# Layer A's queries and keys turned on VectorE as 32-bit pairs of heads, instead of on TensorE

## The chip, the cores and the metric

The kernel runs on one core of one Trainium2 chip. The metric is the device time of one launch in microseconds. The kernel before takes 3019.47 us, the median of three runs from 3016.03 to 3024.8.

## What is computed

Four layers run one after the other on x, a sequence of 2048 rows of 512 values, each with a layer norm ahead and a residual: A, B, A, B. Layer A is recurrent. It works on segments of 32 rows; ahead of each stand 8 memory rows, which are the first 8 output rows of the segment before.

```python
for s in range(n_seg):                      # 64 segments of 32 rows
    h = concatenate([mem, x[:, 32*s:32*s+32]], axis=1)      # 40 rows
    q, k, v = (einsum('btd,dhe->bhte', h, W) for W in (Wq, Wk, Wv))   # 32 heads of 128
    scores = einsum('bhqe,bhke->bhqk', q, k) * scale        # masked, softmax -> p
    o = einsum('bhqk,bhke->bhqe', p, v)
    o = einsum('bhte,hed->btd', o, Wo)
    mem = o[:, :8]
    outs.append(o[:, 8:])
```

Layer B is full softmax attention over the 2048 rows, 32 heads of 16.

## The kernel before, in words

Layer A's 64 segments follow each other, since each needs the memory rows of the one before. What TensorE does beside them is layer B's attention on rows that layer A has finished. The program writes TensorE's order itself: `segment` keeps a list of layer A's steps (`PLAN`, or `PLAN_PAIRS` when five or more units of layer B are due), a clock of its own estimates when each operand will be ready (`Clock`), and `step` picks each time among a step of layer A, a unit of layer B's attention (`emit_qk`, then `pv_mm`), or a piece of a chain (layer norm, projections of layer B). A quota of units, mostly 8 a segment, paces layer B; `PLACE` and `B_PLACE` set the segment positions at which the pieces of chains come due. What is left of layer B's attention when layer A ends runs in a tail, where ScalarE's exponentials are written to a ring (`fill`, L476, three tiles of 512 each, called fills below). Other engines take their instructions in the order in which this program emits them, and `evac_engine` and `evac16` choose VectorE or ScalarE for each copy out of PSUM by the same clock.

One segment, for each half of the heads (rr = 0, 1):

- Projections (`col_steps`, L737). 16 matmuls of 512 columns make Q, K or V of 16 heads. The array is used as four tiles of 32 columns, so four matmuls on different parts of W run side by side, each writing 32 PSUM partitions. Query row q of four heads then stands on partition 32t + q, with the head's 128 values along the free axis.
- The scores need Q and K with the 128 values on the partitions. `stage` copies the PSUM bank to a_qk as bf16 (L324 on ScalarE, L326 on VectorE). `turn` transposes its four pieces of 128x128 on TensorE against the identity into another bank (L761), using the full array. `qk_turn` copies that to a_QT or a_KT (`evac16`, L335 on ScalarE, L337 on VectorE). The steps are named X (Q) and Y (K) in the plan.
- The score group S (`s_group`, L795 and L801) adds the mask and multiplies, 32 matmuls of 40 columns. ScalarE takes the exponential (L805), VectorE sums, divides and transposes the probabilities (L808 to L817).
- `pv_group` or `pv_pair` (P, A, B in the plan, L824) multiplies by V, and `wo_steps` (W, L854) by Wo. L978 copies the memory rows into the next segment's input.

The last 8 rows of four segments are projected together, once in four segments, as a chain (`ln_chunk`): a_qkx, turned eight pieces at a time by the same `turn`, then a_QX and a_KX. GpSimd puts each segment's share into a_QP and a_KT (`rest_place`, L719 and L722).

The units of layer B use the array as four tiles of 32 rows for their first product (L588) and as column tiles for the second (L602). ScalarE takes their exponentials (L590 of three banks, L593 of one).

## Time and profile before

| | |
|---|---|
| median of three runs | 3019.47 us (3016.03 to 3024.8) |
| span of the profiled execution | 3016.9 us |
| TensorE busy | 2793.8 us |
| ScalarE busy | 2296.1 us |
| VectorE busy | 1787.0 us |
| GpSimd busy | 661.3 us |

The profile is of one execution; its own time is the span, from the first to the last instruction. Times are microseconds unless marked ns. PE is TensorE's matmuls, PEld its weight loads, DVE is VectorE, ACT is ScalarE, POOL is GpSimd. Line numbers (L761) are lines of the kernel before; a line can be a helper's, as L326, where every cast on VectorE is recorded. Matmuls are pipelined, so the duration of one (221 ns for a transpose) is longer than the distance to the next, and busy times of groups overlap.

### The profile page before, as it was taken

How to read it: one execution, taken by the hardware profiler on the slowest of the kernel's cores; microseconds unless marked ns; L12 is line 12 of the kernel's file. 1: busy time of each engine (PE TensorE's matmuls, PEld its weight loads, DVE VectorE, ACT ScalarE, POOL GpSimd, SP SyncE). 2: the span in 40 equal slices, each digit the busy share in tenths (PEclk: the TensorE clock that was granted, in tenths of full speed). 3: DMA queues.
4: the chain of work that ended last, by engine and by line, in shares of the span. 5: the costliest groups of instructions: out<-in, count | busy, mean ns of one | idle time of the engine just before them, and what ended most of it. 6: DMA issues, size and time to landing. Idle time of an engine off the chain costs nothing.

```text
span 3016.9 us, 153258 instructions
## 1 busy us (share of the span) xinstructions
PE 2793.8 (93%) x68190; PEld 1702.6 (56%) x68190; DVE 1787.0 (59%) x4836; ACT 2296.1 (76%) x2816; POOL 661.3 (22%) x1165
## 2 busy tenths in 40 slices
PE   5999999999999999999999999999999999998897
PEld 3666565655555555555656655555556555554463
DVE  2344646476666766577766667767666666654302
ACT  2555767587788788667787777778778899899996
POOL 2222222222222222203212212222222122221110
PEclk9999999999999999999999999999999999999998
DMA  6112224243444446435434433544452544555340
GB/s 255 50 47 77 87 82 122 83 136 114 141 123 142 136 118 192 125 106 171 131 99 123 123 91 116 149 140 129 120 170 81 171 125 131 182 168 159 104 120 14
DMA packets 281282, 373.74 MB, mean 124 GB/s; under 512 B 74105, under 2 KB 202305, under 8 KB 279073
## 3 DMA queue, kind: packets, MB, share of 16 engines
q1 hardware_dynamic: 222096, 186.25, 21.9%
q0 software_dynamic: 55040, 168.68, 17.6%
q8 instruction: 535, 8.77, 1.2%
q10 hardware_dynamic: 3472, 8.91, 0.8%
q14 instruction: 139, 1.13, 0.1%
HBM read 260.06 MB, written 103.55 MB: 121 GB/s over the span
## 4 chain that ended last, share of the span: by engine, by line
PE 62%; ACT 14%; DVE 9%; issue 8%; DMA 6%; POOL 1%; SPq 0%; DVEq 0%; ACTq 0%; POOLq 0%
PE bank L737 23%; PE bank L854 12%; ACT b_pr L476 7%; PE b_SX L588 6%; PE b_oacc L602 6%; PE bank L761 4%; ACT b_pt L590 3%; PE bank L824 3%; DMA b_W<-in_B_wqkv_dram 2%; ACT b_pt L593 2%; PE bank L801 1%; PE bank L1237 1%; PE bank L1283 1%; DMA a_Wq<-in_A_Wq_dram 1%; DVE a_qk L326 1%
## 5 line engine op out<-in xcount | busy, mean ns | idle before, releaser
L590 ACT ACTIVATE b_pt<-b_SX 128x1536 bf16<-128x1536 f32 (+1 forms) x877 | 1270.9, 1449 | 384.3 <-PE bank L588 354.6
L593 ACT ACTIVATE b_pt<-bank 128x512 bf16<-128x512 f32 (+1 forms) x877 | 523.2, 597 | 0.6 <-PE bank L588 0.6
L854 PE MATMUL bank<-a_OT,a_Wo 128*128 128x40 bf16 x16384 | 482.0, 180 | 24.3 <-ACT a_OT L324 18.4
L854 PEld LDWEIGHTS <-a_Wo 128*128 128x128 bf16 x16384 | 449.4, 96 | 67.2 <-issue 58.7
L737 PEld LDWEIGHTS <-a_hT 128*32 128x32 bf16 x12288 | 298.0, 96 | 294.9 <-issue 38.5
L588 PE MATMUL b_SX<-b_q,b_k 32*128 32x256 bf16 (+3 forms) x3870 | 353.0, 313 | 21.1 <-ACT b_pt L590 13.8
L588 PE MATMUL bank<-b_q,b_k 32*128 32x512 bf16 (+3 forms) x1290 | 337.0, 312 | 8.4 <-DVE a_V L326 2.5
L602 PE MATMUL b_oacc<-b_pt,b_v 128*17 128x512 bf16 (+3 forms) x5160 | 322.9, 314 | 11.0 <-DVE b_ain L1070 4.3
L326 DVE CAST a_OT<-bank 128x160 bf16<-128x160 f32 x778 | 216.7, 316 | 127.9 <-PE bank L824 125.1
L737 PE MATMUL bank<-a_Wv,a_hT 128*32 128x512 bf16 x4096 | 285.4, 383 | 1.7 <-DVE b_O L1330 1.3
L326 DVE CAST a_qk<-bank 128x512 bf16<-128x512 f32 x338 | 229.5, 681 | 84.2 <-PE bank L737 79.6
L737 PE MATMUL bank<-a_Wk,a_hT 128*32 128x512 bf16 x4096 | 271.8, 382 | 5.3 <-DVE a_hT L978 5.1
L737 PE MATMUL bank<-a_Wq,a_hT 128*32 128x512 bf16 x4096 | 275.5, 381 | 0.7 <-DVE a_V L326 0.4
L476 ACT ACTIVATE b_pr<-b_S 128x1536 bf16<-128x1536 f32 x202 | 270.9, 1876 | 1.1 <-PE b_S L473 1.1
L588 PEld LDWEIGHTS <-b_k 32*128 32x128 bf16 x5160 | 119.2, 91 | 193.7 <-issue 156.0
L1055 POOL DMA_DIRECT2D b_A<-b_ain x176 | 96.2, 546 | 595.8 <-DVE b_ain L1070 403.1
L1070 DVE TENSOR_TENSOR b_ain<-b_oacc,b_ain 128x512 f32<-128x512 f32 (+1 forms) x244 | 165.6, 679 | 91.9 <-PE b_oacc L602 88.0
L602 PEld LDWEIGHTS <-b_v 128*17 128x17 bf16 x6432 | 117.2, 88 | 163.0 <-issue 125.1
L761 PE MATMUL bank<-c_ident,a_qk 128*128 128x128 bf16 x2048 | 179.9, 221 | 23.1 <-DVE a_qk L326 12.7
L824 PE MATMUL bank<-a_PT,a_V 32*128 32x40 bf16 x3472 | 181.0, 177 | 15.3 <-DVE chk L351 3.4
L761 PEld LDWEIGHTS <-a_qk 128*128 128x128 bf16 x2048 | 119.6, 98 | 123.6 <-DVE a_qk L326 49.9
L808 DVE TENSOR_REDUCE a_sm<-a_pn 128x5 f32<-128x200 bf16 x256 | 92.4, 361 | 161.3 <-ACT a_pn L805 157.6
(156 smaller groups left out, 4103.1 us busy)
## 6 DMA issues: line engine op xcount, KB each, us to landing
b_ain<-b_A SPq DMA_DIRECT2D x232, 256.0 KB
b_W<-in_B_wqkv_dram POOLq DMA_DIRECT2D x192, 256.0 KB, 4.0
b_A<-b_ain POOLq DMA_DIRECT2D x176, 256.0 KB, 3.0
b_q<-b_Q SPq DMA_DIRECT2D x252, 128.0 KB
b_k<-b_K SPq DMA_DIRECT2D x199, 128.0 KB
b_v<-b_V SPq DMA_DIRECT2D x306, 68.0 KB
b_A<-b_aout POOLq DMA_DIRECT2D x80, 128.0 KB, 2.8
a_rest<-a_vx POOLq DMA_DIRECT2D x64, 128.0 KB, 2.7
```

The lines of the kernel that those rows point to most:

```text
L326: self.nc.vector.tensor_copy(dst, src)
L476: nc.scalar.activation(self.ring[:, s:s + n, :], self.sets[i][:, 0:n, :], ACT.Exp, scale=B_SCALE)
L588: nc.tensor.matmul(out[t][:, j * qw:(j + 1) * qw], lhsT=k[32 * t:32 * t + 32, kj * 128:(kj + 1) * 128], rhs=q[32 * t:32 * t + 32, j * u.ru ...
L590: nc.scalar.activation(pt[:, 0:NX, 0:w], self.SX[:, 0:NX, 0:w], ACT.Exp, scale=B_SCALE)
L593: nc.scalar.activation(pt[:, NX + i, 0:w], b.t[:, 0:w], ACT.Exp, scale=B_SCALE)
L602: self.nc.tensor.matmul(self.oacc[32 * t:32 * t + 17, j * step:j * step + qw], lhsT=u.v[:, kj, 17 * t:17 * t + 17], rhs=u.p[:, t, j * qw:( ...
L737: self.nc.tensor.matmul(b.t[32 * t:32 * t + 32, :], lhsT=lhsT(ft), rhs=W[:, ft, n * 512:(n + 1) * 512], start=(ft == 0), stop=(ft == 3), t ...
L761: self.nc.tensor.transpose(ps[:, 4 * i + j, :], x[:, 128 * j:128 * j + 128], self.ident[:])
L824: self.nc.tensor.matmul(ps[:, L * h4:L * h4 + L], lhsT=V[32 * t:32 * t + rows, st, h4 * DH:(h4 + 1) * DH], rhs=self.PT[32 * t:32 * t + row ...
L854: self.nc.tensor.matmul(ps[:, ft, :], lhsT=self.Wo[:, h, 128 * ft:128 * ft + 128], rhs=self.OT[:, h, :], start=(h == 0 and ft == 0), stop= ...
L1055: B.k.nc.gpsimd.dma_start(B.Acc_d[self.qc][self.hg][:, self.qo:self.qo + self.qw], acc[:, 0:self.qw])
L1070: nc.vector.tensor_tensor(acc[:, w], k.oacc[:, w], acc[:, w], ALU.add)
```

## The change

The columns of Wq and Wk are read in another order, so that one projection bank holds, on its partitions 32t to 32t + 31, the values 32t to 32t + 31 of 16 heads. The copy from PSUM writes the values of two heads alternately, so that two neighbouring bf16 form one 32-bit word. One VectorE transpose of 256 such words turns each 32x32 block, straight into a_QT, a_KT, a_QX or a_KX, now with two heads interleaved in their last axis. The score group reads Q and K with a step of two elements. The four transposes on TensorE, their PSUM bank and the copy out of it are gone, as are the steps X and Y of the plan; the two plans and the two tables of positions are written anew.

```diff
-PLACE = (-2.0, -1.5, -1.4, -1.4, -1.3, -0.5, -0.4, -0.4, 3.8)
-B_PLACE = (-2.7, -1.4, 0.4, 0.7, 1.7)
+PLACE = (-2.0, -1.6, -1.4, -1.1, -0.8, -0.5, -0.4)
+B_PLACE = (-4.3, -2.3, 0.1, 1.0, 2.1)
...
-        self.QT = bp.tile([128, 2, 4, 4, MAIN], bf16, name="a_QT")
-        self.KT = bp.tile([128, 2, 4, 4, L], bf16, name="a_KT")
+        self.QT = bp.tile([128, 2, 8, MAIN, 2], bf16, name="a_QT")
+        self.KT = bp.tile([128, 2, 8, L, 2], bf16, name="a_KT")
...
         def one(rr, w):
             def then(b, done):
-                t = self.lnp.tile([128, 512], bf16, name="a_qkx", tag="t", bufs=4)
-                b.free = self.evac(t[:], b.t[:], 512, done)
-                qk[w] = (t, b.free)
...
+                at = self.turn((self.QX, self.KX)[w][:, rr].rearrange("p i q b -> p i (q b)"), b, done)
+                if rr and w:
+                    self.at["X", ck] = at
...
-    def col_steps(self, W, lhsT, rr, ready, then):
+    def col_steps(self, W, lhsT, rr, ready, then, turned=False):
         st = {}
+        Wt = W[:].rearrange("p f (r i t c) -> p f r i t c", r=2, t=4, c=32)
...
-                self.nc.tensor.matmul(b.t[32 * t:32 * t + 32, :], lhsT=lhsT(ft), rhs=W[:, ft, n * 512:(n + 1) * 512],
-                                      start=(ft == 0), stop=(ft == 3), tile_position=(0, 32 * t))
+                out, rhs = b.t[32 * t:32 * t + 32, :], W[:, ft, n * 512:(n + 1) * 512]
+                if turned:
+                    out, rhs = out.rearrange("p (i c) -> p i c", c=32), Wt[:, ft, rr, :, t, :]
+                self.nc.tensor.matmul(out, lhsT=lhsT(ft), rhs=rhs, start=(ft == 0), stop=(ft == 3), tile_position=(0, 32 * t))
...
-    def stage(self, b, done):
-        t = self.stp.tile([128, 512], bf16, name="a_qk")
-        b.free = self.evac(t[:], b.t[:], 512, done)
-        return t, b.free
-
-    def turn(self, xs):
-
-        b, at = self.take()
-        ps = b.h(8, 128)
-        for i, (x, _) in enumerate(xs):
-            for j in range(4):
-                self.nc.tensor.transpose(ps[:, 4 * i + j, :], x[:, 128 * j:128 * j + 128], self.ident[:])
-        return b, self.ck.pe(0.224 * len(xs), max([at] + [r for _, r in xs]), "full", 4 * len(xs))
+    def turn(self, dst, b, done):
+
+        x = self.stp.tile([128, 8, 32, 2], bf16, name="a_qk")
+        b.free = self.evac(x[:].rearrange("p i c b -> p i b c"), b.t[:].rearrange("p (i b c) -> p i b c", b=2, c=32), 512, done)
+        self.nc.vector.transpose(dst.bitcast(i32), x[:].bitcast(i32).rearrange("p i c b -> p i (c b)"))
+        return self.ck.ew("DVE", 256, b.free)
...
-                    lhsT = self.QP[:, 4 * rr + t, j, :] if i else self.QT[:, rr, j, t, :]
-                    nc.tensor.matmul(ps[32 * t:32 * t + 32, 4 if i else j, :], lhsT=lhsT, rhs=self.KT[:, rr, j, t, :],
+                    lhsT = self.QP[:, 4 * rr + t, j, :] if i else self.QT[:, rr, 2 * t + j // 2, :, j % 2]
+                    nc.tensor.matmul(ps[32 * t:32 * t + 32, 4 if i else j, :], lhsT=lhsT, rhs=self.KT[:, rr, 2 * t + j // 2, :, j % 2],
...
-    PLAN = "K0 Q0 P1 Q1 Y0 X0 S0 W1 K1 W0 Y1 V0 X1 W3 W2 V1 S1 P0".split()
-    PLAN_PAIRS = "W1 Q0 W3 V0 Y0 K0 A1 X0 S0 X1 V1 K1 Q1 B0 Y1 A0 B1 S1 W0 W2".split()
+    PLAN = "S1 K0 Q0 K1 Q1 S0 W0 P0 W3 V0 V1 W2 P1 W1".split()
+    PLAN_PAIRS = "Q0 S0 K0 A1 B0 W3 K1 W1 Q1 V0 B1 V1 S1 W0 A0 W2".split()
```

`rest_place` keeps its two GpSimd copies, with the new layouts. The score group's masks, the softmax and everything after it are as before.

How the order moves, at two places. The first is TensorE in a segment with eight units (the 51st), from the projection that makes K of the first half (a_Wk) to the next unit of layer B. Before, the four transposes stand in between:

```order
L737 LDWEIGHTS a_hT
L737 MATMUL bank_242<-a_Wk,a_hT 32x512
...
L761 LDWEIGHTS a_qk
L761 MATMUL bank_243<-c_ident,a_qk 128x128
...
L588 LDWEIGHTS b_k
L588 MATMUL b_SX<-b_q,b_k 128x512
```

With the change:

```order
L730 LDWEIGHTS a_hT
L730 MATMUL bank_244<-a_Wk,a_hT 32x512
...
L588 LDWEIGHTS b_k
L588 MATMUL b_SX<-b_q,b_k 128x512
...
L602 LDWEIGHTS b_v
L602 MATMUL b_oacc<-b_pt,b_v 17x512
...
L771 LDWEIGHTS c_ident
L771 MATMUL bank_243<-c_hide,c_ident 32x200
```

The unit (L588, L602) follows the projection directly, and the score group (L771) comes after it.

The second place is VectorE in the same segment, from the first cast of Q or K to the first softmax. Before:

```order
L326 CAST a_qk<-bank_243 128x512
L1063 COPY b_aout<-b_oacc 128x256
L326 CAST a_V<-bank_244 128x512
L326 CAST a_qk<-bank_242 128x512
L337 COPY a_QT<-bank_243 128x512
L1070 TENSOR_TENSOR b_ain<-b_oacc,b_ain 128x512
L337 COPY a_KT<-bank_245 128x16x32
L326 CAST a_V<-bank_242 128x512
L808 TENSOR_REDUCE a_sm<-a_pn 128x5
```

With the change:

```order
L326 CAST a_qk<-bank_242 128x8x2x32
L746 STREAM_TRANSPOSE a_QT<-a_qk 128x256
L1031 COPY b_aout<-b_oacc 128x256
L326 CAST a_qk<-bank_243 128x8x2x32
L746 STREAM_TRANSPOSE a_KT<-a_qk 128x8x32
L326 CAST a_qk<-bank_244 128x8x2x32
L746 STREAM_TRANSPOSE a_KT<-a_qk 128x8x32
L784 TENSOR_REDUCE a_sm<-a_pn 128x5
```

Each cast is followed by its transpose, the copies out of the second bank are gone, and the two casts of V have left VectorE's queue here for ScalarE's.

## Rows read from the trace of the kernel before

**Rows 1.** The page's busy times: us, share of the span, instructions.
```profile
PE 2793.8 (93%) x68190; PEld 1702.6 (56%) x68190; DVE 1787.0 (59%) x4836; ACT 2296.1 (76%) x2816; POOL 661.3 (22%) x1165
```

**Rows 2.** Busy time of each engine in four stages of the span.
```profile
core 0: us, PE busy (x) PEld busy (x) DVE busy (x) ACT busy (x) POOL busy (x), PEclk, DMA share, GB/s
0.00:400.00 400.00, 345.95 (x9589) 225.34 (x9592) 177.55 (x539) 211.59 (x400) 90.14 (x163) 0.99 0.31 102
400.00:2400.00 2000.00, 1903.75 (x47839) 1156.89 (x47832) 1339.22 (x3593) 1525.03 (x1891) 469.51 (x823) 0.99 0.43 128
2400.00:2700.00 300.00, 282.36 (x6621) 161.76 (x6621) 188.69 (x493) 272.12 (x309) 65.98 (x116) 0.98 0.48 144
2700.00:3017.00 317.00, 261.79 (x4153) 158.57 (x4148) 81.50 (x212) 287.34 (x220) 35.64 (x63) 0.97 0.37 109
```

**Rows 3.** The chain that ended last: shares of the span by line.
```profile
by line: PE bank L737 22.9%; PE bank L854 12.3%; issue 8.2%; ACT b_pr L476 6.9%; PE b_SX L588 6.5%; PE b_oacc L602 5.5%; PE bank L761 4.2%; ACT b_pt L590 3.5%; PE bank L824 2.7%; DMA b_W<-in_B_wqkv_dram 2.2%; ACT b_pt L593 1.7%; PE bank L80
```

**Rows 4.** The same chain in order of time, one segment: start, length, what.
```profile
1003.53 1.29 PE bank L737 x24
...
1006.57 0.33 PE bank L761 x4
...
1007.88 0.98 PE bank L737 x16
...
1008.94 0.23 PE bank L801 x32
1009.17 0.32 PE b_SX L588 x3
...
1009.50 0.32 PE b_oacc L602 x4
...
1012.42 0.54 PE b_oacc L602 x8
1012.96 0.55 PE bank L761 x8
```

**Rows 5.** Groups by form, TensorE's transposes: busy us, mean ns; idle before, releaser.
```profile
L761 PE MATMUL bank<-c_ident,a_qk 128*128 128x128 bf16 x2048 | 179.9, 221 | 23.1 <-DVE a_qk L326 12.7 <-DVE a_xo L1204 5.3 <-ACT a_QX L335 3.4
L761 PE MATMUL bank<-c_ident,a_qkx 128*128 128x128 bf16 x512 | 39.6, 220 | 0.9 <-ACT a_qkx L324 0.7 <-issue 0.2
```

**Rows 6.** The same view, copies, casts and transposes on VectorE and ScalarE.
```profile
L326 DVE CAST a_qk<-bank 128x512 bf16<-128x512 f32 x338 | 229.5, 681 | 84.2 <-PE bank L737 79.6 <-ACT b_pt L590 0.2
L326 DVE CAST a_V<-bank 128x512 bf16<-128x512 f32 x204 | 140.3, 688 | 73.0 <-PE bank L737 72.1
L815 DVE STREAM_TRANSPOSE a_PT<-a_pn 128x256 bf16<-128x256 bf16 x256 | 113.7, 444 | 7.9
L337 DVE COPY a_KT<-bank 128x512 bf16<-128x512 bf16 x222 | 92.4, 416 | 68.5 <-PE bank L761 67.3
L337 DVE COPY a_QT<-bank 128x512 bf16<-128x512 bf16 x223 | 92.3, 414 | 4.1 <-ACT b_pt L593 3.0 <-PE bank L761 0.6
L337 DVE COPY a_KX<-bank 128x512 bf16<-128x512 bf16 x64 | 26.9, 420 | 46.4 <-PE bank L761 45.0
L326 DVE CAST b_vst<-bank 128x512 bf16<-128x512 f32 x32 | 21.7, 678 | 39.4 <-PE bank L1283 37.1 <-issue 1.1 <-ACT b_pt L590 1.0
L335 ACT COPY a_KT<-bank 128x512 bf16<-128x512 bf16 x34 | 20.1, 590 | 3.4 <-PE bank L761 3.3
L337 DVE COPY a_QX<-bank 128x512 bf16<-128x512 bf16 x47 | 19.4, 414 | 0.0
```

**Rows 7.** Source view of L761: what its engine was idle for.
```profile
its engine sat idle before it (us, times) until:
  DVE a_qk L326: 62.6, 163
```

**Rows 8.** Groups by form, the tail's exponentials on ScalarE.
```profile
L476 ACT ACTIVATE b_pr<-b_S 128x1536 bf16<-128x1536 f32 x201 | 270.4, 1879 | 1.1 <-PE b_S L473 1.1
```

More of the change, by code (lines that the diff above doesn't have):

```diff
@@ L129, in __init__ @@
         self.ring, self.stream, self.slot, self.fills, self.summed, self.more = None, deque(), 0, 0, 0, True
-        self.staged, self.pos, self.placed = {}, 0.0, -1
+        self.pos, self.placed = 0.0, -1
         self.first_xn, self.rush = None, False
@@ L691, in rest @@
             return self.col_steps(self.Wv, lambda ft: self.hX[:, ft, :], rr, self.w_at["V"], then)
-        qk = {}
         def one(rr, w):
             def then(b, done):
-                t = self.lnp.tile([128, 512], bf16, name="a_qkx", tag="t", bufs=4)
-                b.free = self.evac(t[:], b.t[:], 512, done)
-                qk[w] = (t, b.free)
-            return self.col_steps((self.Wq, self.Wk)[w], lambda ft: self.hX[:, ft, :], rr, max(self.at["x"], self.w_at["QK"[w]]), then)
-        def turn(rr):
-            b, done = self.turn((qk[1], qk[0]))
-            ps = b.h(8, 128)
-            self.evac16(self.KX[:, rr].rearrange("p j t q -> p j (t q)"), ps[:, 0:4], 512, done)
-            b.free = self.evac16(self.QX[:, 4 * rr:4 * rr + 4].rearrange("p t j q -> p t j q"), ps[:, 4:8].rearrange("p j (t q) -> p t j q", q=32), 512, done)
-            if rr:
-                self.at["X", ck] = b.free
-            return b.free
+                at = self.turn((self.QX, self.KX)[w][:, rr].rearrange("p i q b -> p i (q b)"), b, done)
+                if rr and w:
+                    self.at["X", ck] = at
+            return self.col_steps((self.Wq, self.Wk)[w], lambda ft: self.hX[:, ft, :], rr, max(self.at["x"], self.w_at["QK"[w]]), then, turned=True)
         plan = [4 * ck + x for x in PLACE] if ck else ()
         v = [lambda: rest(0), lambda: rest(1)]
-        x = [lambda: one(0, 0), lambda: one(0, 1), lambda: turn(0), lambda: one(1, 0), lambda: one(1, 1), lambda: turn(1)]
-        c = self.chain([pe] + (x + v if late else v + x), self.ck.t["PE"] + wait, modes="fccfccfcc" if late else "fccccfccf", plan=plan, gate=(6, 4 * ck - 1))
-        c.v_left = 1 if late else 7
+        x = [lambda: one(0, 0), lambda: one(0, 1), lambda: one(1, 0), lambda: one(1, 1)]
+        c = self.chain([pe] + (x + v if late else v + x), self.ck.t["PE"] + wait, modes="fcccccc", plan=plan, gate=(4, 4 * ck - 1))
+        c.v_left = 1 if late else 5
         return c
@@ L748, in cols @@
         return out
[L750 to L762 removed]
+    def turn(self, dst, b, done):
[3 more added lines that the diff above has]
+        return self.ck.ew("DVE", 256, b.free)
     def qk_steps(self, h_s, proj, rr):
         def then(b, done):
[L766 to L776 removed]
+            self.at["X", proj, rr] = self.turn((self.QT[:, rr], self.KT[:, rr, :, 0:MAIN, :])[proj].rearrange("p i q b -> p i (q b)"), b, done)
+        return self.col_steps((self.Wq, self.Wk)[proj], lambda ft: h_s[:, ft, :], rr, max(self.at.get("mem", 0.0), self.w_at["QK"[proj]]), then, turned=True)
     def v_steps(self, h_s, rr):
@@ L867, in a_ready @@
             t = max(at.get("mem", 0.0), self.w_at[k])
-        elif k in "XY":
-            p = "QK"[k == "Y"]
-            if f"{p}{g}" in left:
-                return INF
-            t = self.staged[p, g][1]
         elif k == "S":
-            if f"X{g}" in left or f"Y{g}" in left or at["R"] == INF:
+            if f"Q{g}" in left or f"K{g}" in left or at["R"] == INF:
                 return INF
@@ L887, in a_ready @@
         return max(t, self.bank_at())
-    MODE = {"Q": "PV", "K": "PV", "X": "full", "Y": "full", "S": "PV", "V": "PV", "P": "S", "A": "S", "B": "S", "W": "full"}
+    MODE = {"Q": "PV", "K": "PV", "S": "PV", "V": "PV", "P": "S", "A": "S", "B": "S", "W": "full"}
     def a_pick(self, left):
```

26 lines of the change are left out of this document (6 added, 20 removed).

## The prediction

> **What bounds the kernel now.** I read the busy shares first. TensorE is busy for 93% of the span, ScalarE for 76%, VectorE for 59% [rows 1]. A share over the whole span hides the stages, so the next view is the table by stage [rows 2]. In the first 400 us, where layer A runs almost alone, and from 400 to 2400 us, where units of layer B's attention are woven in, TensorE is busy 86% and 95% and ScalarE 53% and 76%. From 2400 to 2700 us ScalarE has come up to 91% and TensorE stands at 94%. After 2700 us, when layer A is over and only exponentials of layer B are left, ScalarE leads with 91%. So until about 2700 us the order in which TensorE gets through its list sets the time, and after that ScalarE does. The chain that ended last says the same: the projections (L737) and the output product (L854) lead it, and the transposes of Q and K (L761) hold 4.2% of it [rows 3], 127 us of 3016.9.
>
> The chain in order of time shows the price of one place [rows 4]. Four transposes stand for 0.33 us, eight for 0.55 us. So four more cost 0.22 us, and the remaining 0.11 us is what a change of the array's tiling costs (full array for transposes, column tiles for projections, row tiles for the units). Projections go at 0.98 us for 16, that is 0.245 for four matmuls with the change, and at 1.29 for 24, that is 0.215.
>
> **The change, part by part.**
>
> *Transposes on TensorE go.* 2048 of them on a_qk and 512 on a_qkx [rows 5], 640 fours at 0.22 us: **-141 us**.
>
> *Changes of tiling go.* Counted over TensorE's two orders up to the first fill of the tail, neighbours with different tilings fall from 3109 to 2637, because most fours stood between two projections or between a projection and a unit. 472 at 0.11 us: **-52 us**. Together 193 us. The bounds: the chain counts only 127 us, since some fours stood where something else was late anyway; the busy time of the two groups is 219.5 us [rows 5], which overlaps its neighbours. I take 193, the price at which the engine was seen to advance, and keep 127 and 219 as ends. The order shows no work put in the hole: the same projections and score groups follow, closer together.
>
> *The copies out of PSUM go, and VectorE transposes come.* 640 copies go, 556 of them on VectorE (222 + 223 + 64 + 47) at about 0.415 us, the other 84 on ScalarE at 0.59 [rows 6]. 640 transposes of 256 words come, all on VectorE. No row has a transpose of 32-bit words. The nearest is that of 256 bf16 elements, 0.444 us [rows 6]; below it stands a copy of 512 values at 0.414, above it twice the row, 0.89, if a 32-bit word should count as two. I take 0.444: 284 us come and 231 go. The orders also hand 97 casts of V from VectorE to ScalarE, 97 x 0.688 [rows 6] = 67 us off VectorE and 57 us on ScalarE, which loses 84 x 0.59 = 50 us of copies. Both engines end near where they were, and TensorE's path pays nothing while VectorE is at 67% in the long stage [rows 2]. If that cover goes, score groups wait: the second rival.
>
> *The cast with its values interleaved.* 640 casts keep their count of 512 and write every second bf16. The cast into b_vst writes in pieces of 16 and takes 0.678 us against 0.681 for the plain one [rows 6]. I take zero; twice the time would put 0.68 us on an engine that is not the bound.
>
> *The wait that is added.* A transpose follows its cast in VectorE's queue, and where the cast is on ScalarE (245 of 640) VectorE waits for another engine with softmax rows behind it. The orders put the softmax of an earlier score group ahead of such a transpose, so I price this at zero and leave it to the second rival. The waits before the old transposes, 62.6 us of weight-load idling on VectorE's a_qk [rows 7], may vanish or move to the score groups; on TensorE's own row only 23.1 us stood before them [rows 5]. I take "moves", and -23 us as the end.
>
> *Operands read with gaps.* Score groups read Q and K with a step of two elements, projections read Wq and Wk in 16 runs of 32 columns. No row has either. Taken as free; the bounds are in the third rival and, for the 256 score groups, 0.23 us once more each [rows 4], 59 us, if such a read ran at half pace.
>
> *Work that moves to the tail.* The new order runs 842 units beside layer A where the old one ran 865, 15 of the 23 missing in layer A's last 16 segments, and 232 fills in the tail instead of 201.3. This takes 23 x 2 x 0.21 us (four more matmuls of a unit's second product, 0.54 against 0.33 us [rows 4]) from TensorE's list, **-10 us**, and puts 30.7 fills of 270.4/201 = 1.345 us [rows 8] on ScalarE where ScalarE is the bound, **+41 us**.
>
> *ScalarE comes closer.* From 400 to 2400 us its 1525 us of work stay and the stage shrinks by some 140 us, so its share goes from 76 to about 82%. In the stage where it is at 91% TensorE's share is 1.1 points lower than in the long one [rows 2]. Between nothing and twice those 1.1 points of 2000 us, 44 us, I take **+20 us**.
>
> The sum is -141 - 52 - 10 + 41 + 20 = -142 us. The profiled execution spans 3016.9 us, 2.6 us under the median of the three runs, 3019.47; from the median the forecast is **2878 us**.
>
> **The rivals.**
>
> *ScalarE takes a large part back.* For it: 91% in the last stage, and segments that come without layer B's projections have the least TensorE work for the same eight units, so there ScalarE would end last. Against it: in the long stage it has a quarter to spare. Then TensorE's list gives only what the chain counted: 127 + 10 - 41 - 20 = 76 us, 2943 us.
>
> *VectorE is late with K and Q.* If a 32-bit transpose takes 0.89 us, or waits as long behind a cast on ScalarE, each of 256 score groups starts up to 0.44 us later, 113 us in all; 2991 us. For it: both transposes and the two casts of a group now stand in one queue, and the score group follows the last projection at a distance of one or two groups. Against it: VectorE's 67%. The Trainium skill speaks for this side too: "VectorE: DVE Perf Modes", Rules for kernel authors, says to transpose 128x128 on TensorE where a PSUM destination will do. The trace disagrees as far as it goes, since the engine that the page recommends is the one at 93%.
>
> *Slower: the projections' operand.* Each of the 2560 fours of matmuls on Wq and Wk now reads 16 runs of 32 columns instead of one of 512. If a run cost as much as four short matmuls of the score group, 0.23/8 = 0.029 us [rows 4], a four would take 0.46 us in place of 0.215 and the kernel 627 us more, 3505 us. It decides from 142/2560 = 0.055 us per four, a quarter more than now. For it: no row shows such a read. Against it: four projections that read at four addresses at once already run at 0.215 us for 512 columns, so the reads have slack in where they go. The Trainium skill bears on this: "SBUF — State Buffer", Door 1, says lines are 16 bytes and two hits in each suffice for full rate. By that rule neither the runs of 64 bytes nor the step of 4 bytes costs anything; no run here shows it.
>
> **How the numbers follow.** The forecast's own case, 2828 to 2915 us, has 0.62: its lower end takes 219 us for the transposes, no loss to ScalarE and the 23 us of waits (2878 - 26 - 20 - 23 is 2809, of which I keep the part that can come together). ScalarE's case has 0.20 and reaches to about 2970; VectorE's has 0.08; the projections' 0.07; that something else eats it all has 0.03. The range 2828 to 2950 holds the first and most of the second, 0.8 in all. About 0.3%, 9 us, is what a measurement of this kernel can tell from no change. Faster by more: 0.62 + 0.20 + 0.07 = 0.89. The same: 0.03. Slower: 0.08.
>
> **What would show it.** Right: no L761 rows; fours of projections still 0.215 us apart in the chain; 640 transposes on VectorE at about 0.44 us; layer A over some 180 us earlier, near 2520 us; 232 fills behind it, the tail 40 us longer; ScalarE near 82% in the long stage. ScalarE's case would show as PE waiting for b_pt or free b_SX before the units, VectorE's as score groups waiting for a_QT or a_KT, the projections' as a chain step above 0.27 us for four. The forecast is wrong if layer A's end comes less than 120 us earlier, or if the tail grows by more than 60 us.

## The result and the profile after

The changed kernel takes **2910.72 us**, the median of four runs (2906.69 to 2912.67), beside 3021.62 us for the kernel before, with one run more than the three ahead (3016.03 to 3024.8). The ratio is 0.9627, with an interval of 0.961 to 0.9644, a gain of some 111 us where 142 were forecast. The profiled execution spans 2908.7 us, 108.2 less than the span of before.

The page's busy times, engine by engine, answer to [rows 1]:

```profile
PE 2645.1 (91%) x65859; PEld 1586.6 (55%) x65859; DVE 1741.4 (60%) x4758; ACT 2335.4 (80%) x2876; POOL 667.4 (23%) x1165
```

TensorE lost 149 us of busy time. ScalarE has 39 us more work in a span that is 108 us shorter, and that is the first thing that was not in the forecast: there its casts and copies came to 57 - 50 = 7 us more, and the fills of the tail only do exponentials that units did beside layer A before.

The table of stages, cut where layer A's parts now end, answers to [rows 2]; its columns are as there:

```profile
0.00:400.00 400.00, 341.62 (x9931) 218.21 (x9934) 207.97 (x625) 219.84 (x391) 95.00 (x171) 0.98 0.32 104
400.00:2200.00 1800.00, 1677.01 (x43252) 997.90 (x43245) 1219.59 (x3323) 1463.39 (x1846) 448.02 (x778) 0.98 0.45 133
2200.00:2550.00 350.00, 328.03 (x8001) 189.10 (x7997) 228.76 (x594) 324.25 (x393) 85.29 (x148) 0.98 0.50 151
2550.00:2909.00 359.00, 298.42 (x4705) 181.40 (x4701) 85.05 (x218) 327.90 (x249) 39.08 (x69) 0.97 0.36 106
```

In the long stage TensorE has gone from 95% to 93% (1677 of 1800) and ScalarE from 76% to 81%. In the stage ahead of the tail they stand together, 94% and 93%. The granted clock in the long stage reads 0.98 where it read 0.99.

The chain that ended last, by line, answers to [rows 3]:

```profile
by line: PE bank L730 18.6%; PE bank L830 12.9%; issue 12.7%; ACT b_pr L476 7.8%; PE b_SX L588 5.7%; ACT b_pt L590 5.5%; PE b_oacc L602 4.8%; ACT b_pt L593 2.8%; PE bank L800 2.4%; DVE a_qk L326 1.8%; PE bank L1205 1.4%; DMA b_W<-in_B_wqkv_
```

The transposes (L761, 4.2%) are gone and nothing of TensorE stands in their place. The projections' own pace is as in [rows 4], 24 of them in 1.29 us, in the same chain in order of time:

```profile
917.11 1.29 PE bank L730 x24
```

Of the chain's work, what grew most is ScalarE's exponentials of layer B's units, L590 and L593, from 3.5 + 1.7 to 5.5 + 2.8 per cent, and a cast of Q and K on VectorE (L326) has come in with 1.8. What grew more than any work is "issue", time in which the engine that the chain passes through waited for nothing that the profile shows: 8.2 to 12.7 per cent, some 120 us. Its longest piece, 15.93 us from 1918.97, stands where the chain passes through GpSimd's queue. TensorE's own idle time grew by far less (below), so these shares say where the chain runs and not what was lost there.

Where layer A ends is seen from the source view of the copy of the memory rows, the last instruction of each segment. Before, and then after (min/median/max in ns, first and last start in us):

```profile
L978 DVE CAST a_hT<-bank x126: 178/191/192, 58.5 to 2679.2; 128x32 bf16<-128x32 f32 x126
```
```profile
L946 DVE CAST a_hT<-bank x126: 129/192/193, 54.8 to 2531.7; 128x32 bf16<-128x32 f32 x126
```

Layer A's last such copy comes 147.5 us earlier. From it to the end of the span it was 3016.9 - 2679.2 = 337.7 us and is now 2908.7 - 2531.7 = 377.0, so the tail grew by 39.3 us. The forecast had 183 us earlier and 41 us longer. All that it missed lies inside layer A.

Busy times up to that last copy, before and then after (columns as in [rows 2]):

```profile
0.00:2679.20 2679.20, 2512.76 (x63519) 1532.41 (x63523) 1694.04 (x4589) 1988.88 (x2574) 624.54 (x1100) 0.99 0.42 126
0.00:2531.70 2531.70, 2329.00 (x60734) 1395.12 (x60734) 1644.16 (x4506) 1990.12 (x2606) 626.13 (x1092) 0.98 0.44 131
```

So TensorE's busy time in layer A fell by 184 us, and its idle time (the stretch less the busy time) grew from 166.4 to 202.7, by 36 us. The forecast's terms for TensorE's work were -141 - 52 - 10 = -203, and +20 was its term for ScalarE coming closer, which would show as idle time. Of the 35 us that layer A ended too late, 19 are busy time that stayed and 16 are more idle time than forecast.

The groups by form show the new price of the casts and transposes; they answer to [rows 6], and the last row to [rows 8]:

```profile
L476 ACT ACTIVATE b_pr<-b_S 128x1536 bf16<-128x1536 f32 x232 | 312.1, 1895 | 3.5 <-PE b_S L473 3.4
L326 DVE CAST a_qk<-bank 128x512 bf16<-128x512 f32 x395 | 287.1, 727 | 81.6 <-PE bank L730 79.3
L324 ACT CAST a_qk<-bank 128x512 bf16<-128x512 f32 x245 | 183.1, 752 | 52.9 <-PE bank L730 45.2
...
L746 DVE STREAM_TRANSPOSE a_KT<-a_qk 128x256 int32<-128x256 int32 x256 | 113.0, 443 | 45.6 <-ACT a_qk L324 40.1
L746 DVE STREAM_TRANSPOSE a_QT<-a_qk 128x256 int32<-128x256 int32 x256 | 111.8, 437 | 24.7 <-ACT a_qk L324 20.1
L324 ACT CAST a_V<-bank 128x512 bf16<-128x512 f32 x149 | 89.6, 613 | 22.1 <-PE bank L730 21.4
```

For ScalarE's casts [rows 6] had no row; the same view of the kernel before has it:

```profile
L324 ACT CAST a_qk<-bank 128x512 bf16<-128x512 f32 x174 | 102.6, 590 | 58.1 <-PE bank L737 57.9
L324 ACT CAST a_V<-bank 128x512 bf16<-128x512 f32 x52 | 30.5, 586 | 13.8 <-PE bank L737 11.3 <-ACT a_pn L805 1.6
```

Two things are to be read here. The transpose of 256 words of 32 bits takes 0.443 and 0.437 us, what one of 256 bf16 took. The cast that writes every second bf16 is not free: 0.752 us on ScalarE against 0.590 for the plain one, 0.727 on VectorE against 0.681. That is 245 x 0.162 = 40 us more on ScalarE and 395 x 0.046 = 18 us on VectorE.

What TensorE's weight loads and matmuls were idle for is in the source views, of the units' first product (L588) and of the score group (L801, now L777). Before, the units, then the score group:

```profile
  ACT b_pt L590: 13.8, 47
...
  ACT b_pt L593: 1.7, 8
```
```profile
  ACT a_QT L335: 4.9, 13
  DVE a_QT L337: 3.1, 12
  DVE a_KT L337: 1.5, 8
```

After, in the same order:

```profile
  ACT b_pt L590: 30.4, 85
...
  ACT b_pt L593: 5.2, 23
```
```profile
  DVE a_QT L746: 24.3, 24
  DVE a_KT L746: 9.6, 22
```

The units wait for ScalarE 35.6 us instead of 15.5. The score groups wait for K and Q 33.9 us instead of 9.5. The source view adds up the idle time of two rows, matmuls and weight loads, and a weight load's idle time can lie beside a matmul. By this view the old transposes had 62.6 us ahead of them for VectorE's a_qk alone [rows 7], and 24.4 us more have come ahead of the score groups. By the row of matmuls alone 23.1 us stood ahead of the old transposes on a_qk [rows 5], and the score groups' first matmuls have 14.6 where L801 had 0.6:

```profile
L777 PE MATMUL bank<-a_KT,a_QT 128*32 128x40 bf16 x4096 | 71.1, 182 | 14.6 <-DVE a_QT L746 8.4 <-DVE ln_mv L372 3.5 <-DVE a_KT L746 2.0
```

So part of these waits moved to the score groups, about six tenths by the matmuls' row and four tenths or less by both rows.

The last view is TensorE's granted clock, the mean of each execution (before, then after):

```profile
core 0: 3016.9 us, clock 0.987
```
```profile
core 0: 2908.7 us, clock 0.981
```

The clock has two levels, 2.4 and 1.2 GHz, which the rows give as 1 and 0.5; a mean below 1 tells of stretches at the lower one. Stretches at 0.5 cost at most half of their length directly, which for a whole execution is one less the mean, times the span: 0.013 x 3016.9 = 39 us before, 0.019 x 2908.7 = 55 us after. Two of the falls, in the table of the stretches ahead of each and behind it (columns as in [rows 2]):

```profile
917.90:927.90 10.00, 8.59 (x176) 4.05 (x172) 9.05 (x24) 9.57 (x13) 3.45 (x6) 1.00 0.43 134
928.00:931.30 3.30, 3.30 (x80) 2.61 (x72) 3.20 (x11) 2.38 (x4) 2.04 (x4) 0.50 0.74 242
1576.70:1586.70 10.00, 8.33 (x336) 5.49 (x334) 6.80 (x21) 9.70 (x14) 1.67 (x4) 1.00 0.54 154
1586.80:1590.10 3.30, 3.30 (x114) 3.00 (x107) 1.18 (x5) 1.48 (x2) 0.54 (x1) 0.50 0.34 92
```

Ahead of each fall TensorE was busy for 8.6 and 8.3 of 10 us while ScalarE was busy for 9.6 and 9.7: TensorE was idle in small pieces, the longest wait 0.9 us in both stretches, in the first for VectorE's b_ain and in the second for ScalarE's b_pt. Behind it TensorE runs at 1.2 GHz, with no idle time left, until the clock comes back.

### The profile page after: what moved, and what is told of

It reads as the page before. It is cut to its first block, busy times and chain, and to the rows that moved or that the text cites. A ratio compares the mean times of both kernels' runs of the same rounds, so it can differ in the third digit from the quotient of the medians.

```text
span 2908.7 us, 148110 instructions
## 1 busy us (share of the span) xinstructions
PE 2645.1 (91%) x65859; PEld 1586.6 (55%) x65859; DVE 1741.4 (60%) x4758; ACT 2335.4 (80%) x2876; POOL 667.4 (23%) x1165
## 4 chain that ended last, share of the span: by engine, by line
PE 51%; ACT 18%; issue 13%; DVE 9%; DMA 5%; POOL 3%; POOLq 0%; DVEq 0%; ACTq 0%; SPq 0%
PE bank L730 19%; PE bank L830 13%; ACT b_pr L476 8%; PE b_SX L588 6%; ACT b_pt L590 5%; PE b_oacc L602 5%; ACT b_pt L593 3%; PE bank L800 2%; DVE a_qk L326 2%; PE bank L1205 1%; DMA b_W<-in_B_wqkv_dram 1%; DMA b_A<-b_ain 1%; PE bank L777 1%; ACT a_qk L324 1%; DVE ln_st L370 1%
## 5 line engine op out<-in xcount | busy, mean ns | idle before, releaser
L590 ACT ACTIVATE b_pt<-b_SX 128x1536 bf16<-128x1536 f32 (+1 forms) x854 | 1245.2, 1458 | 285.2 <-PE bank L588 261.3
L593 ACT ACTIVATE b_pt<-bank 128x512 bf16<-128x512 f32 (+1 forms) x854 | 516.7, 605 | 7.0 <-PE bank L588 7.0
L830 PE MATMUL bank<-a_OT,a_Wo 128*128 128x40 bf16 x16384 | 476.4, 180 | 22.1 <-issue 11.2
L730 PEld LDWEIGHTS <-a_hT 128*32 128x32 bf16 x12288 | 316.2, 96 | 283.2 <-issue 36.1
L588 PE MATMUL b_SX<-b_q,b_k 32*128 32x256 bf16 (+3 forms) x3732 | 344.9, 316 | 36.6 <-ACT b_pt L590 30.4
L588 PE MATMUL bank<-b_q,b_k 32*128 32x512 bf16 (+3 forms) x1244 | 329.8, 315 | 18.8 <-DVE b_xo L1339 7.5
L326 DVE CAST a_qk<-bank 128x512 bf16<-128x512 f32 x395 | 287.1, 727 | 81.6 <-PE bank L730 79.3
L602 PE MATMUL b_oacc<-b_pt,b_v 128*17 128x512 bf16 (+2 forms) x4976 | 317.9, 317 | 11.4 <-DVE b_ain L1038 4.7
L476 ACT ACTIVATE b_pr<-b_S 128x1536 bf16<-128x1536 f32 x232 | 312.1, 1895 | 3.5 <-PE b_S L473 3.4
L326 DVE CAST a_OT<-bank 128x160 bf16<-128x160 f32 x736 | 203.1, 313 | 179.1 <-PE bank L800 175.7
L730 PE MATMUL bank<-a_Wv,a_hT 128*32 128x512 bf16 x4096 | 270.3, 381 | 1.7 <-DVE a_xo L1172 1.2
L588 PEld LDWEIGHTS <-b_k 32*128 32x128 bf16 x4976 | 119.2, 92 | 255.9 <-issue 226.3
L324 ACT CAST a_qk<-bank 128x512 bf16<-128x512 f32 x245 | 183.1, 752 | 52.9 <-PE bank L730 45.2
L602 PEld LDWEIGHTS <-b_v 128*17 128x17 bf16 x6432 | 118.8, 89 | 168.0 <-issue 130.8
L195 POOL DMA_DIRECT2D b_W<-in_B_wqkv_dram x192 | 145.7, 761 | 245.2 <-PE bank L1205 125.0
L800 PEld LDWEIGHTS <-a_V 32*128 32x128 bf16 x4096 | 126.0, 91 | 101.3 <-issue 53.6
```

Source lines behind the costliest of these rows:

```text
L195: self.nc.gpsimd.dma_start(t[:], self.WB_src[:, :, col:col + 256])
L324: self.nc.scalar.copy(dst, src)
L326: self.nc.vector.tensor_copy(dst, src)
L476: nc.scalar.activation(self.ring[:, s:s + n, :], self.sets[i][:, 0:n, :], ACT.Exp, scale=B_SCALE)
L588: nc.tensor.matmul(out[t][:, j * qw:(j + 1) * qw], lhsT=k[32 * t:32 * t + 32, kj * 128:(kj + 1) * 128], rhs=q[32 * t:32 * t + 32, j * u.ru ...
L590: nc.scalar.activation(pt[:, 0:NX, 0:w], self.SX[:, 0:NX, 0:w], ACT.Exp, scale=B_SCALE)
```

## The experiments

Each kernel is compared by its ratio to the kernel before on the same chip, since the kernel before itself took 3021.62 to 3034.35 us on the chips used. Edits are against the changed kernel where nothing else is said.

**The cast, plain.** The cast writes its 512 values in a row, so that a word holds two neighbouring values of one head. Q and K are then in another order, and the scores are of other values.

```diff
-b.free = self.evac(x[:].rearrange("p i c b -> p i b c"), b.t[:].rearrange("p (i b c) -> p i b c", b=2, c=32), 512, done)
+b.free = self.evac(x[:].rearrange("p i c b -> p (i c b)"), b.t[:], 512, done)
```

> The changed kernel with one edit: the cast out of PSUM writes its 512 values in a row instead of every second bf16 (so Q and K hold their values in another order than the scores need; nothing else is left out). Theory A, the interleaved write is what the forecast missed: the cast of a_qk took 0.752 us on ScalarE and 0.727 on VectorE in the changed kernel, against 0.590 and 0.681 before; with the plain write they go back to those, 245 x 0.16 = 39 us leave ScalarE and 395 x 0.046 = 18 us VectorE, and since ScalarE paces the units the time falls by 20 to 40 us from 2910.7, to 2870 to 2890. Rival B, the casts lie beside other work and the missing 32 us went into waits of the new order (score groups close behind their projections): the casts get shorter, the time stays within 9 us of 2910.7.

**The cast, reading with gaps.** The interleaving is moved to the other side: the cast reads PSUM with a step of 32 words and writes in a row. The result is that of the change.

```diff
-b.free = self.evac(x[:].rearrange("p i c b -> p i b c"), b.t[:].rearrange("p (i b c) -> p i b c", b=2, c=32), 512, done)
+b.free = self.evac(x[:], b.t[:].rearrange("p (i b c) -> p i c b", b=2, c=32), 512, done)
```

> The changed kernel, but the cast reads PSUM with a step of 32 words and writes in a row (same result). If the cost lies in writing single bf16 with gaps, the casts go back to 0.59 and 0.68 us and the time goes where the plain cast's goes (theory A: 2870 to 2890; B: 2911). If any order with gaps costs the same on either side, the casts stay at 0.75 and 0.73 us and the time at 2911.

Measured: 2910.18 us, ratio 0.9577 (0.9548 to 0.9606), for the plain cast, and 2902.31 us, 0.9559 (0.9527 to 0.959), for the one that reads with gaps. Groups by form of the first and of the second:

```profile
L326 DVE CAST a_qk<-bank 128x512 bf16<-128x512 f32 x395 | 266.4, 675 | 85.8 <-PE bank L730 83.5
L324 ACT CAST a_qk<-bank 128x512 bf16<-128x512 f32 x245 | 144.9, 592 | 67.2 <-PE bank L730 67.1
```
```profile
L326 DVE CAST a_qk<-bank 128x512 bf16<-128x512 f32 x395 | 266.3, 674 | 83.5 <-PE bank L730 81.3
L324 ACT CAST a_qk<-bank 128x512 bf16<-128x512 f32 x245 | 144.9, 592 | 68.9 <-PE bank L730 68.1 <-PE bank L777 0.6
```

Gaps on the side that reads PSUM cost nothing, 592 and 674 ns, and gaps on the side that writes cost all of the difference. The kernel that reads with gaps does what the change does and is the fastest of this study: run again later it took 2899.32 us, 0.9561 (0.9544 to 0.9577), beside the change's 0.9627 (0.961 to 0.9644) and, in another run of it, 0.9618 (0.9596 to 0.9641). 0.0057 to 0.0068 of some 3030 us is 17 to 21 us for the interleaved write, with some 10 us of uncertainty by the intervals. The change and this kernel were never timed on the same chip. By their own times, 2910.72 and 2916.06 against 2902.31 and 2899.32, it is 8 to 17 us, and layer A's last copy comes at 2520.3 and 2525.2 us instead of 2531.7 and 2535.9, 11 us earlier in the mean. So the write costs **some 8 to 21 us**, a fifth to a half of the 40 us that it adds to ScalarE. The plain cast comes out lower: 0.0041 to 0.0050, 12 to 15 us, by the ratio, and nothing by its own time beside the change's first run. By the first it lies between its two expectations, by the second it is the rival's.

**Gaps in the projections' output or operand.** Could the projections interleave, and the cast be plain? In the first kernel they write PSUM with a step of two words, in the second they read the columns of W one by one, 256 bytes apart. Both use the plain cast.

```diff
-out, rhs = out.rearrange("p (i c) -> p i c", c=32), Wt[:, ft, rr, :, t, :]
+out, rhs = out.rearrange("p (i c b) -> p i b c", b=2, c=32), Wt[:, ft, rr, :, t, :].rearrange("p (i b) c -> p i b c", b=2)
```

> The changed kernel, but the projections of Q and K write PSUM with a step of two words, so that two heads are interleaved there already and the cast is plain (same result). If TensorE writes with that step at its full pace (fours of matmuls 0.215 us apart), the time is that of the plain cast. If the step costs TensorE, it shows in the distance of the fours: a half more, 0.11 us on 2560 fours, would be 275 us more than the plain cast, some 3160.

```diff
-out, rhs = out.rearrange("p (i c) -> p i c", c=32), Wt[:, ft, rr, :, t, :]
+out, rhs = out.rearrange("p (i c b) -> p i c b", b=2, c=32), Wt[:, ft, rr, :, t, :].rearrange("p (i b) c -> p i c b", b=2)
```

> The changed kernel, but the projections of Q and K read the weights' columns in the interleaved order (neighbouring columns 256 bytes apart), write PSUM in a row, and the cast is plain (same result). If TensorE reads single columns at any address at its full pace, the time is that of the plain cast. The third rival of the prediction in its hardest form: if such reads cost, a four takes up to twice 0.215 us, 2560 x 0.215 = 550 us more than the plain cast, some 3430.

Measured: 3378.99 us, ratio 1.112 (1.1086 to 1.1153), and 3504.59 us, 1.1541 (1.1507 to 1.1574). The source views of the projections (duration min/median/max in ns) of the change, of the first and of the second kernel:

```profile
L730 PE MATMUL bank<-a_Wk,a_hT x4096: 376/379/634, 39.0 to 2535.4; 128*32 128x512 bf16 x196
```
```profile
L730 PE MATMUL bank<-a_Wk,a_hT x4096: 592/634/1142, 41.4 to 2999.3; 128*32 128x512 bf16 x196
```
```profile
L730 PE MATMUL bank<-a_Wk,a_hT x4096: 642/644/662, 40.1 to 3121.0; 128*32 128x512 bf16 x196
```

The change's own operand, 16 runs of 64 bytes, costs nothing: 376/379/634 is word for word what L737 had. What the third rival priced is real, but it starts at single columns, not at runs: 644 ns, and the kernel then takes 3505 us, by chance the very figure of that rival. The rule that the prediction cited from the Trainium skill ("SBUF — State Buffer", Door 1: lines of 16 bytes, two hits in each for full rate) holds on both sides of this: runs of 64 bytes and steps of 4 bytes pass, steps of 256 bytes do not. For the written side, the Trainium skill's "PSUM — Partial Sum Buffer", Specifications (TRN2), says that PSUM's lines are 8 bytes and that an access which is not contiguous slows matmuls significantly; the 634 ns for every second word agree.

**Which engine is near the path?** Three kernels add work to one engine each, around Q and K (the second and third thereby also make Q and K later): four matmuls of 128 columns over the full array ahead of each projection bank of Q and K (so the 640 fours are back, without the copies), each VectorE transpose twice, and each of ScalarE's casts of Q and K twice. They were timed beside another run of the change (2916.06 us, 0.9618, 0.9596 to 0.9641; clock 0.979).

```diff
+            if turned and ft == 0:
+                for j in range(4):
+                    self.nc.tensor.matmul(b.t[:, 128 * j:128 * j + 128], lhsT=self.ident[:], rhs=self.ident[:], start=True, stop=True)
```

> The changed kernel with four matmuls of 128 columns on the full array put back on TensorE ahead of each projection of Q and K (identity times identity, overwritten by the projection; 640 fours, nobody waits for them, the order is that of the changed kernel). Their work on TensorE is 640 x 0.22 = 141 us and one or two more changes of tiling each, 0.11 us, 70 to 141 us: 211 to 282 us. Theory A, TensorE still sets the pace of layer A: nearly all of it shows, 190 us or more over the changed kernel. Rival B, ScalarE has taken over in most segments: less than half shows, under 130 us.

Measured: 3118.56 us, ratio 1.0289 (1.0271 to 1.0306), 202 us over the change: over the 190 of theory A, though under the 211 us that the expectation had as the least work added. Counted as in the prediction, this kernel has 3712 changes of tiling up to the first fill where the change has 2637, so besides 640 fours there are 1075 changes more. At the prices of [rows 4], 0.22 and 0.11, that is 259 us; 202 are 0.78 of it. TensorE's busy time in layer A grew by 234 us (2330.8 to 2564.8) and its idle time fell from 205.1 to 168.6, about the 166.4 of the kernel before. So TensorE's list still sets the pace, and what is added to it is in part taken out of its waits.

```diff
         self.nc.vector.transpose(dst.bitcast(i32), x[:].bitcast(i32).rearrange("p i c b -> p i (c b)"))
+        self.nc.vector.transpose(dst.bitcast(i32), x[:].bitcast(i32).rearrange("p i c b -> p i (c b)"))
```

> The changed kernel with each VectorE transpose of Q and K issued twice, 640 more at about 0.37 to 0.44 us, 237 to 284 us of work on VectorE and 0.4 us more before each score group can start. Theory A, VectorE has room (60% busy) and score groups can wait: under 60 us more. Rival (the prediction's VectorE case), score groups stand too close behind their projections: 0.4 us at each of 256 groups, 100 us or more.

Measured: 3027.3 us, ratio 0.9986 (0.9973 to 0.9999), 111 us over the change. VectorE's busy time grew by 218 us (1740.6 to 1958.9), so half of it shows, near the 113 us of the prediction's second rival. What the score groups of this kernel waited for:

```profile
  DVE a_KT L747: 136.1, 171
  DVE a_QT L747: 58.5, 58
```

33.9 us have become 194.6. VectorE, at 60% over the span, is near the path at the one place where K and Q are made.

```diff
+        eng = self.evac_engine(512, done)
+        if eng == "ACT":
+            self.nc.scalar.copy(x[:].rearrange("p i c b -> p i b c"), b.t[:].rearrange("p (i b c) -> p i b c", b=2, c=32))
```

> The changed kernel with those casts of Q and K that go to ScalarE issued twice, 245 more at about 0.64 us from start to start, 157 us of work on ScalarE during layer A. Theory A (TensorE sets the pace, ScalarE has a fifth to spare): under 50 us more. Rival B (ScalarE sets the pace in most segments): 100 us or more.

Measured: 3065.29 us, ratio 1.0101 (1.0084 to 1.0118), 149 us over the change for 158 us of work on ScalarE (2335.9 to 2493.8). The idle time of the units in this kernel, and of its score groups:

```profile
  ACT b_pt L590: 74.5, 122
```
```profile
  DVE a_QT L749: 97.1, 98
```

The units wait for ScalarE 44 us more than in the change (30.4). But the score groups wait for Q and K 108.3 us (11.2 of it for a_KT) instead of 33.9, 74 us more: the added copy stands ahead of the cast, so Q and K come later by its length. The edit loads ScalarE and delays Q and K at once, and its 149 us are not the price of a busier ScalarE alone.

All three of these edits cost time, so work on no one engine around Q and K is free in the changed kernel. ScalarE's edit looked the dearest, at 0.94 of its work, and the next question was whether that is new.

**The same on the kernel before.** Each of ScalarE's 238 casts of Q and K (174 of a_qk, 64 of a_qkx) issued twice, in the kernel before; the copies behind the transposes (L335) stay single. The edit of a_qk is shown, that of a_qkx is the same:

```diff
+        eng = self.evac_engine(512, done)
+        if eng == "ACT":
+            self.nc.scalar.copy(t[:], b.t[:])
         b.free = self.evac(t[:], b.t[:], 512, done)
```

> The kernel before, with every copy and cast that ScalarE makes of Q and K in the first layer issued twice: 238 more instructions of about 0.48 us start to start, some 114 us of ScalarE work. Theory (the change moved the bound: before it ScalarE had room, TensorE alone set the pace): well under half of it shows, 0 to 50 us over the kernel before. Rival (ScalarE was as near to the path before as it is after the change, where the same edit showed at 0.95 of the added work): 90 to 110 us over the kernel before.

Measured: 3087.52 us, ratio 1.0188 (1.0152 to 1.0223), 57 us for 124 us of work (2296.1 to 2419.7). That is 0.46 of the work, between the two expectations: clear of the rival's 90, while its interval, 46 to 68 us, takes in the theory's end of 50. ScalarE had some room before, less than I had given it. Here too the edit delays Q and K: the transposes wait for ScalarE's a_qk 66.5 us instead of 11.4, the units for b_pt 26.5 instead of 13.8.

The granted clock may hold much of the difference between 149 and 57. Here are the runs with the mean granted clock of their profiled execution, the most that stretches at 1.2 GHz can have cost in it directly, as worked out above, and TensorE's busy and idle time up to layer A's last copy:

| kernel | span, us | clock | cost of stretches at 0.5, at most, us | TensorE in layer A, busy + idle, us |
|---|---|---|---|---|
| before | 3016.9 | 0.987 | 39 | 2512.8 + 166.4 |
| before, ScalarE's casts twice | 3082.0 | 0.984 | 49 | 2534.8 + 210.2 |
| the change, two profiles | 2908.7; 2915.0 | 0.981; 0.979 | 55; 61 | 2329.0 + 202.7; 2330.8 + 205.1 |
| cast that reads with gaps | 2904.5 | 0.978 | 64 | 2328.9 + 196.3 |
| fours back on TensorE | 3114.2 | 0.985 | 47 | 2564.8 + 168.6 |
| VectorE's transposes twice | 3023.0 | 0.974 | 79 | 2365.7 + 279.5 |
| ScalarE's casts twice | 3066.0 | 0.956 | 135 | 2392.1 + 295.8 |
| V on VectorE (below) | 2961.3 | 0.962 | 112 | 2359.1 + 238.2 |
| ScalarE counted dearer (below) | 2980.2 | 0.954 | 137 | 2380.9 + 234.2 |

ScalarE's casts twice put up to 135 - 61 = 74 us of this on the change and 49 - 39 = 10 us on the kernel before. (On its own chip the kernel before ran at 0.981 to 0.985, about 48 us, and there the edit put nothing on it.) With all of it taken off, 149 us would be 75 and 57 would be 47 to 57, which is 0.47 and 0.38 to 0.46 of the work added, much nearer to each other. That the clock is the difference is not shown: these are upper ends, and for nearly the same matmuls TensorE's busy time in layer A grew by 61 us on the change, its idle time by 91. The edits that raised the clock are those that gave TensorE more to do: the fours (0.985 against 0.979), and the two kernels whose projections have gaps (0.986 and 0.989).

**Work from ScalarE to VectorE.** If ScalarE alone stood at the bound, moving work off it should gain. The program shares out each copy by its own estimates, so both edits move other casts and units too: with V sent to VectorE, 95 casts of V leave ScalarE, 26 others (11 of Q and K, 15 of a_vx) come to it, and its busy time falls by 25 us, not by 57. Both kernels start from the cast that reads with gaps (its second run is their base); the first raises the number by which the sharing of copies counts ScalarE's work dearer, the second sends the casts of V alone to VectorE in segments with six or more units.

> The kernel whose cast reads PSUM with gaps and writes in a row, once more, on the chip on which the next two are timed: 0.954 to 0.96 of the kernel before by the run made earlier. It is the base of the next two.

```diff
-        self.act_bias = 0.6 if quota >= 6 else 0.0
+        self.act_bias = 2.0 if quota >= 6 else 0.0
```

> The kernel whose cast reads with gaps, with the number that counts ScalarE's work dearer in the sharing of copies raised from 0.6 to 2.0 for the first layer's units: some 44 casts of Q and K, 95 of V and 81 of the attention output go from ScalarE to VectorE, about 220 instructions of 0.6 us or 130 us of ScalarE work. Theory (ScalarE is at the bound and VectorE has room): 20 to 60 us faster than the base. Rival (VectorE, which the score groups now wait for, is as near): no gain, or up to 40 us slower than the base.

```diff
-            b.free = self.at["V", rr] = self.evac(self.V[:, rr, :], b.t[:], 512, done)
+            b.free = self.at["V", rr] = self.evac(self.V[:, rr, :], b.t[:], 512, done, "DVE" if self.act_bias else None)
```

> The kernel whose cast reads with gaps, with the casts of V alone sent to VectorE where the sharing counts ScalarE's work dearer: some 95 casts of 0.6 us, about 57 us, go from ScalarE to VectorE. Theory (ScalarE at the bound): 10 to 40 us faster than the base. Rival (VectorE as near): within 5 us of the base, or slower by up to 25 us.

Measured: the base 2899.32 us; ScalarE counted dearer 2983.34 us, 0.9836 (0.9813 to 0.986), **84 us slower**; V on VectorE 2950.92 us, 0.9723 (0.9697 to 0.9748), **52 us slower**. The theory fell, and so did the size that its rival gave, twice over. The source views of the base (units, score group, product with V):

```profile
  ACT b_pt L590: 25.9, 74
```
```profile
  DVE a_QT L746: 20.9, 19
  DVE a_KT L746: 7.7, 19
```
```profile
  DVE a_V L326: 20.7, 37
  ACT a_V L324: 14.9, 33
  DVE a_PT L793: 5.9, 8
```

The same three of the kernel with V on VectorE:

```profile
  ACT b_pt L590: 48.5, 103
```
```profile
  DVE a_KT L746: 27.9, 40
  DVE a_QT L746: 24.3, 20
```
```profile
  DVE a_V L326: 34.1, 68
...
  DVE a_PT L793: 15.5, 15
```

Score groups wait 52.2 us instead of 28.6, the products with V wait longer for the probabilities, and the units wait 22.6 us more for an engine that has 25 us less to do (2277.7 against 2302.3 busy). And the mean clock goes from 0.978 to 0.962, which is 112 - 64 = 48 us at most where the kernel lost 52; for the other kernel it is 73 at most where it lost 84. The stretch in which one such fall lies, in the kernel with V on VectorE:

```profile
778.10:788.10 10.00, 6.67 (x182) 3.79 (x176) 8.37 (x26) 7.83 (x12) 3.31 (x8) 1.00 0.63 196
788.20:791.50 3.30, 3.30 (x79) 2.06 (x78) 2.71 (x7) 2.18 (x3) 2.12 (x4) 0.50 0.76 189
```

VectorE was busy for 8.4 of the 10 us ahead, TensorE for 6.7. A busy share alone does not tell of a fall: in the same kernel TensorE was busy for 8.23 of the 9.9 us from 771.3, and the 3.3 us behind them ran at 1.00. What is shown is that these waits and these falls come together. The table gives their parts. Layer A became longer by 72 us with V on VectorE and by 90 with ScalarE counted dearer, of which TensorE's idle time, the waits, is 42 and 38; the busy time, where slower matmuls would show, is 30 and 52, less than the 48 and 73 that the clock has at most. The units that these two kernels run in layer A instead of the tail (222 and 224 fills against 232) gave some 15 us back there: the tail took 364 and 365 us instead of 379.

## Why the prediction held, and what it missed

The forecast was 2878 us, the time is 2910.72, in the range and 4 us from the upper end of the likeliest case. By its own steps:

*Transposes and changes of tiling, -141 and -52.* Right in kind, and perhaps too large by a tenth to a fifth. With the fours back on TensorE the kernel lost 202 us, inside the 127 and 219 kept as bounds, but that edit adds more changes of tiling than the change had taken out (1075 against 472), and the prices of [rows 4] make 259 of it. In layer A TensorE's busy time fell by 184 us where these two terms and the -10 make 203. Of the two parts only the sum was measured.

*Copies and VectorE transposes, 0.* Held in size: the 32-bit transpose took 0.443 and 0.437 us against 0.444 taken, and VectorE's busy time went from 1787 to 1741 us. But the cover that I named for it, VectorE at 67%, is thin. Doubling the transposes showed 111 of 218 us, through the wait that the second rival named. That rival was wrong about the price of a word, and right about the place. The rule that the prediction set beside it (the Trainium skill, "VectorE: DVE Perf Modes", Rules for kernel authors) is for a transpose of 128x128; VectorE turns blocks of 32x32 here, so the rule does not bear on the change.

*The cast with its values interleaved, 0.* **This step failed.** The row it was taken from, a cast that writes in pieces of 16, was not near enough to one that writes every second element: 0.752 against 0.590 us on ScalarE. "Twice the time would put 0.68 us on an engine that is not the bound" put a bound on VectorE alone and did not ask about the 245 casts on ScalarE, where they stand in one queue with the exponentials that the units wait for. Taking it away returned some 8 to 21 us.

*The waits, "moves".* Held in part: by the row of matmuls 23.1 us ahead of the old transposes went and 14.0 came ahead of the score groups. The 62.6 us that the prediction called weight-load idling [rows 7] are both rows together; 49.9 of them are weight loads' and 12.7 matmuls'.

*Operands read with gaps, 0.* Held. Projections 379 ns as before, score groups 181 against 179; the third rival fell.

*Work that moves to the tail, -10 and +41.* Held: 232 fills, and the tail grew by 39.3 us.

*ScalarE comes closer, +20.* Its share in the long stage came out at 81% against 82 forecast, and the units' wait for it grew by 20.1 us (15.5 to 35.6). The mechanism is there. That the size agrees is in part luck: +20 was the middle of a guess from a difference of shares, 5 us of the wait are the interleaved cast's own, since with the cast that reads with gaps it stands at 25.9 for L590 instead of 30.4, and all of TensorE's idle time in layer A grew by 36.

So layer A's end came 147.5 us earlier, not 183, and 35 us are to be accounted for, 16 as idle time and 19 as busy time of TensorE. The interleaved cast holds some 8 to 21 of them by its own runs. The granted clock, which the forecast left as it was, has 55 - 39 = 16 us at most. The two are different losses, since the clock stayed at 0.978 when the cast was mended. The rest has two candidates, the clock and a price of the fours that was too high; both would show as busy time, and no run tells them apart: none raised the clock alone.

By the time alone the case is not decided: 2910.72 lies halfway between the forecast's 2878 and the 2943 of ScalarE's case. Two small readings in the prediction are off. "Near 2520 us" for layer A's end fits 180 us ahead of the stages' border at 2700; from the last copy at 2679.2, 183 us earlier is 2496. And in the chances of "faster" the 0.07 of the projections' case stands where the 0.08 of VectorE's belongs (2991 is faster, 3505 slower), so the sums are 0.90 and 0.07.

*The rivals.* ScalarE's case gave 2943 us, the gain shrunk to the 76 us that the chain left. The gain is 111, and the fours put back cost 202, so TensorE's list gave more than that; but the case's sign, units that wait for b_pt, is in the trace, and it came about halfway true. The case that ends slower rested on an operand whose reads cost nothing here.

## What to carry to other kernels

Where a second engine works close behind the one that sets the pace, price an operand's new layout on each engine that may run it, and from a row with the same step between elements, not merely with smaller pieces; if one side of a copy must have gaps, try the side that reads PSUM. A gain on the engine that sets the pace is paid back in part as its idle pieces grow: 36 us here, and about as much came back when the work was put back. TensorE may pay twice, since the granted clock fell behind stretches with such pieces: read the mean clock beside the busy shares, before and after. An edit that doubles an instruction loads its engine and delays its result, so look at who waits before calling it the price of the load. An engine's share over the span (VectorE's 60%) says nothing of room at the one place where another engine waits for it.

## What was not expected of the hardware

- A cast of 512 values from PSUM that writes every second bf16 takes 0.752 us on ScalarE and 0.727 on VectorE; writing in a row, it takes 0.592 and 0.674, whether it reads PSUM in a row or with a step of 32 words.
- A VectorE transpose of 256 words of 32 bits takes what one of 256 bf16 takes, 0.44 us.
- A projection of 512 columns that writes every second word of PSUM goes from 379 to 634 ns; one that reads single columns 256 bytes apart, to 644. Runs of 32 columns, and steps of two elements in the score groups' operands, cost nothing.
- TensorE's granted clock fell to 0.5 with no long wait ahead of it, only short ones of at most 0.9 us: in the two falls shown of the changed kernel TensorE had been busy for 8.3 and 8.6 of the 10 us ahead. With work moved from ScalarE to VectorE the mean clock went from 0.978 to 0.962 and 0.954, and the time by 52 and 84 us.
